# Later read-back of row sums with q and k loaded two pairs ahead, and finished high and low weight parts kept in memory for batches 2 to 4

## The chip, the core and the metric

The kernel runs on one core of a Trainium2 chip. The metric is the time of one execution in microseconds (us), as the device counts it. PE is the matrix engine (TensorE), DVE the vector engine, ACT the scalar engine, POOL is GpSimd, and SP is the engine whose queue issues all of this kernel's DMAs, in program order. Each engine works through its own instruction list in order. A waiting instruction holds up everything behind it on that engine; on SP a waiting DMA issue holds up all later DMAs.

## What is computed

Attention over 4 batches, 12 heads, 448 rows and 64 columns, and then two dense blocks on the result, all in float32 (shortened from the reference):

```
attn = softmax(causal(q @ k.T / 8)) @ v          # q, k, v: (4, 12, 448, 64)
x    = attn.transpose(0, 2, 1, 3).reshape(4, 448, 768)
gate = sigmoid(causal 5-tap convolution of x with conv_w)
x    = (gate * (x @ w_val)) @ w_out              # both 768 x 768
theta = x @ w_theta
y    = w_tok_r @ (x * cos(theta)) + w_tok_i @ (x * sin(theta))   # mixes the 448 rows
u    = x + y
out  = u + relu(u @ w_ch)
```

The weights and `conv_w` arrive as 64-bit floats, 384 KB for a tile of 128 x 384 numbers, and have to be turned into 32-bit numbers in the kernel.

## The kernel before

**Precision.** PE multiplies in a reduced float32 form, so each operand is split into a high part (the value rounded to that form) and a low part (the remainder). Each product is three matmuls: high x high, low x high, high x low.

**Attention** (`attn_iter`) runs head by head; two heads of one batch form a pair `g`, 24 pairs in all, 6 in a batch. For each head it makes scores in four row blocks (`attn_S`), takes the exponential on ACT with the row sums beside it, transposes the probabilities (`attn_PT`), and for each pair multiplies with v (`attn_AV`). `attn_R` (lines 368 to 381) takes the reciprocal of the row sums on DVE, writes these 896 numbers to DRAM (`rows<-rec`, line 375), and at once issues two loads that read them back, spread over all partitions, into a tile `rb` (`rb<-rows`, line 378). `attn_X1` multiplies the product with `rb` (line 389), and `attn_X2` makes the convolution gate. One head is five steps of a generator; `attn_R(g)` is in the fourth step of a pair's second head, `attn_AV(g)` six steps later, `attn_X(g)` four steps after that. The q and k of pair g + 1 are loaded in the second step of pair g's first head, into two buffers each.

**The dense part** (`dense(b)`) of a batch is four stages of six weight groups (`gemm`, lines 440 to 458): `w_val`, `w_out`, `w_theta`, `w_ch`. A group is 128 output columns: two weight tiles of 128 x 384 (g = 0 and 1) and 18 matmuls of 448 columns. Between `w_theta` and `w_ch` come sine and cosine on ACT, transposes (`ztr`) and the token matmuls (`tok`, line 545). The dense part of batch b runs while the attention of batch b + 1 is interleaved with it; the table `RATE` says how many attention steps go with each dense step. The attention of batch 1 runs alone at the start, and the dense part of batch 4 alone at the end. Two groups of batch 1 are multiplied early (`AHEAD`).

**Weights.** In batch 1 a tile is loaded as raw 64-bit numbers (`load_w` into `cv_raw`, four buffers, for group n + 4 while group n is multiplied), converted by three DVE instructions and one on ACT (`to_f32`, in `stage_w`, for group n + 2), written once to DRAM as one float32 tile of 192 KB (`scratch<-w_raw`, line 210), and split by POOL into high (`pool_hi`, line 104) and low (`pool_lo`, line 107, or DVE, line 110) in `split_w`, for group n + 1. In batches 2 to 4 `stage_w` only reads the 192 KB tile back from `scratch` (`w_raw<-scratch`, line 212, three buffers), and `split_w` splits it again on POOL or DVE into `w_hi` and `w_lo` (three buffers each). `W_DVE` says for each batch and stage which low parts DVE makes.

**Order.** All this is written in one stream; a scheduler then orders each engine's list by its own estimate of when things are ready. An `issue_after` block keeps the instructions in it behind a given one on the same engine.

## Time and profile before

| | before |
|---|---|
| time, median of 3 runs | 846.46 us (843.69 to 851.68) |
| profiled execution: its time | 848.2 us |
| profiled execution: span of the trace | 845.7 us |
| PE busy with matmuls | 732.9 us, 87% of the span |
| PE weight loads | 611.6 us, 72% |
| DVE busy | 521.2 us, 62% |
| POOL busy | 515.9 us, 61% |
| ACT busy | 414.1 us, 49% |
| moved by DMA | 88.28 MB, mean 104 GB/s |
| granted PE clock, mean | 0.938 of full speed |

Busy shares are means over stages with different limits, so the kernel is read by stage: the attention of batch 1 (0 to 126 us of the span), the dense part of batch 1 (126 to 342), of batch 2 (342 to 530), of batch 3 (530 to 718) and of batch 4 (718 to 846). PE carries the work that must be done; what a stage can lose is the time in which PE is idle or runs at the lower of its two clocks (1.2 instead of 2.4 GHz; a granted clock of 1.00 is the higher one).

### The profile page before, as it was taken

How to read it: one execution, taken by the hardware profiler on the slowest of the kernel's cores; microseconds unless marked ns; L12 is line 12 of the kernel's file. 1: busy time of each engine (PE TensorE's matmuls, PEld its weight loads, DVE VectorE, ACT ScalarE, POOL GpSimd, SP SyncE). 2: the span in 40 equal slices, each digit the busy share in tenths (PEclk: the TensorE clock that was granted, in tenths of full speed). 3: DMA queues.
4: the chain of work that ended last, by engine and by line, in shares of the span. 5: the costliest groups of instructions: out<-in, count | busy, mean ns of one | idle time of the engine just before them, and what ended most of it. 6: DMA issues, size and time to landing. Idle time of an engine off the chain costs nothing.

```text
span 845.7 us, 12489 instructions
## 1 busy us (share of the span) xinstructions
PE 732.9 (87%) x3965; PEld 611.6 (72%) x3965; DVE 521.2 (62%) x1161; ACT 414.1 (49%) x982; POOL 515.9 (61%) x589
## 2 busy tenths in 40 slices
PE   6577589888397896999889898989989999999997
PEld 4446358666296785878768786868778787898996
DVE  6775698979878562744747644725637834436641
ACT  6667465545567642435558632525558621125311
POOL 3566559667434656577768745567848348676322
PEclk9879669999599898999989999999989999999999
DMA  9984743768534343444423224345332113433113
GB/s 223 185 146 85 139 89 106 206 174 176 181 91 107 61 119 102 82 125 100 101 57 82 52 69 108 89 118 98 84 92 49 32 49 103 132 112 84 36 31 102
DMA packets 151277, 88.28 MB, mean 104 GB/s; under 512 B 93455, under 2 KB 150317, under 8 KB 151213
## 3 DMA queue, kind: packets, MB, share of 16 engines
q1 hardware_dynamic: 151213, 87.51, 42.8%
q8 instruction: 31, 0.51, 0.3%
q14 instruction: 33, 0.27, 0.1%
HBM read 72.45 MB, written 15.03 MB: 103 GB/s over the span
## 4 chain that ended last, share of the span: by engine, by line
PE 47%; DMA 21%; DVE 18%; issue 4%; ACT 4%; POOL 3%; SPq 2%; ACTq 0%; POOLq 0%; DVEq 0%
PE ps_mm L452 23%; PE ps_mm L545 10%; DMA rows<-rec 7%; PE ps_av L357 4%; DMA w_raw<-scratch 4%; PE ps_tr L334 3%; DMA cv_raw<-in_moe_w_val_dram 3%; DMA cv_raw<-in_moe_w_ch_dram 2%; PE ps_s L313 2%; DMA cv_raw<-in_moe_w_theta_dram 2%; DVE w_raw L159 2%; DVE ps_s L315 2%; PE ps_s L314 2%; DVE gate L415 2%; PE ps_tr L531 1%
## 5 line engine op out<-in xcount | busy, mean ns | idle before, releaser
L104 POOL TENSOR_SCALAR w_hi<-w_raw 128x384 fp32r<-128x384 f32 x188 | 113.6, 605 | 151.1 <-PE ps_mm L452 90.1
L452 PE MATMUL ps_mm<-act_hi,w_lo 128*128 128x448 f32 x432 | 163.0, 378 | 8.3 <-POOL w_lo L107 6.4
L452 PE MATMUL ps_mm<-act_hi,w_hi 128*128 128x448 f32 x432 | 163.6, 381 | 6.5 <-POOL w_hi L104 2.1
L107 POOL TENSOR_TENSOR w_lo<-w_raw,w_hi 128x384 fp32r<-128x384 f32 x146 | 157.2, 1078 | 9.3
L452 PE MATMUL ps_mm<-act_lo,w_hi 128*128 128x448 f32 x432 | 159.9, 370 | 0.0
L115 ACT ACTIVATE prob<-ps_s,negm 112x112 f32<-112x112 f32 x192 | 95.2, 497 | 88.3 <-DVE negm L315 86.4
L315 DVE CUSTOM_DVE_ANT_0 ps_s<-ps_s,mask 112x112 f32<-112x112 f32 x192 | 85.6, 454 | 65.1 <-PE ps_s L314 54.4
L334 PE MATMUL ps_tr<-ident,prob 112*112 112x112 f32 x480 | 85.2, 280 | 19.0 <-ACT prob L115 13.1
L452 PEld LDWEIGHTS ps_mm<-act_hi,w_lo 128*128 128x128 f32 x432 | 82.9, 192 | 19.4 <-POOL w_lo L107 10.1
L452 PEld LDWEIGHTS ps_mm<-act_hi,w_hi 128*128 128x128 f32 x432 | 82.4, 192 | 16.0 <-POOL w_hi L104 4.0
L313 PE MATMUL ps_s<-kk,qs 128*112 128x256 f32 x192 | 74.0, 389 | 20.2 <-ACT prob L115 10.3
L452 PEld LDWEIGHTS ps_mm<-act_lo,w_hi 128*128 128x128 f32 x432 | 82.9, 192 | 5.5
L334 PEld LDWEIGHTS ps_tr<-ident,prob 112*112 112x112 f32 x480 | 59.3, 142 | 34.2 <-ACT prob L115 17.9
L107 POOL TENSOR_TENSOR act_lo<-x2f,act_hi 128x448 fp32r<-128x448 f32 x36 | 44.9, 1247 | 53.9 <-DVE act_hi L464 28.4
L347 ACT COPY pt<-ps_tr 112x448 f32<-112x448 f32 (+2 forms) x120 | 51.4, 441 | 48.3 <-PE ps_tr L334 47.6
L357 PE MATMUL ps_av<-pt,v_raw 112*64 112x336 f32 (+3 forms) x384 | 66.4, 451 | 1.7 <-ACT pt L347 1.3
L314 PE MATMUL ps_s<-klo,qs 128*112 128x256 f32 x192 | 62.8, 339 | 3.3 <-DVE klo L110 3.1
L545 PE MATMUL ps_mm<-wtok_h,zt_h 128*128 128x448 f32 x168 | 64.4, 383 | 0.5 <-ACT zt_h L536 0.4
L545 PE MATMUL ps_mm<-wtok_h,zt_l 128*128 128x448 f32 x168 | 63.6, 379 | 1.4 <-DVE zt_l L110 1.3
L545 PE MATMUL ps_mm<-wtok_l,zt_h 128*128 128x448 f32 x168 | 62.0, 369 | 0.0
L411 POOL TENSOR_TENSOR gate<-gate,tp 128x448 f32<-128x448 f32 x48 | 58.8, 1225 | 2.4
L313 PEld LDWEIGHTS ps_s<-kk,qs 128*112 128x112 f32 x192 | 36.7, 192 | 29.1 <-ACT prob L115 12.3
(101 smaller groups left out, 1518.3 us busy)
## 6 DMA issues: line engine op xcount, KB each, us to landing
w_raw<-scratch SPq DMA_DIRECT2D x144, 192.0 KB, 2.4
scratch<-w_raw SPq DMA_DIRECT2D x48, 192.0 KB, 2.8
q_raw<-in_q_dram SPq DMA_DIRECT2D x48, 112.0 KB, 3.0
k_raw<-in_k_dram SPq DMA_DIRECT2D x48, 112.0 KB, 3.3
v_raw<-in_v_dram SPq DMA_DIRECT2D x24, 224.0 KB, 3.2
rb<-rows SPq DMA_DIRECT2D x48, 112.0 KB, 3.3
out_dram<-o SPq DMA_DIRECT2D x24, 224.0 KB, 2.7
cv_raw<-in_moe_w_val_dram SPq DMA_DIRECT2D x12, 384.0 KB, 4.7
```

Of the source, the lines that this page charges most:

```text
L104: nc.gpsimd.tensor_scalar(out=dst, in0=src, scalar1=1.0, scalar2=0.0, op0=ALU.mult, op1=ALU.add)
L107: nc.gpsimd.tensor_tensor(out=dst, in0=src, in1=f32(hi), op=ALU.subtract)
L115: exps.append(nc.scalar.activation(*args, **kw))
L313: nc.tensor.matmul(pt[:CP, :nn], lhsT=qs[:, cs], rhs=kk[:, :nn], start=True, stop=False)
L314: nc.tensor.matmul(pt[:CP, :nn], lhsT=qs[:, cs], rhs=klo[:, :nn], start=False, stop=True)
L315: ttr = nc.vector.tensor_tensor_reduce(out=pt[:CP, :n], in0=pt[:CP, :n], in1=mask[:, S - n : S], scale=-1.0 / math.sqrt(D), scalar=3.0e38, ...
L334: nc.tensor.transpose(pt[:CP, off : off + CP], prob[i, c][:, kc * CP : (kc + 1) * CP], ident[:CP, :CP])
L347: nc.scalar.copy(t, src)
L357: nc.tensor.matmul(av[g][j * D : (j + 1) * D, kc * CP : S], lhsT=tv[:, j, kc, :], rhs=pT.pop((2 * g + j, kc)), start=kc == 0, stop=kc == N ...
L411: nc.gpsimd.tensor_tensor(out=gt, in0=gt, in1=tp, op=ALU.add)
L452: nc.tensor.matmul(pt[:, :S], lhsT=a[:, kc % KH, :], rhs=x, start=kc == 0 and m == 0, stop=kc == KC - 1 and m == 2,)
L545: nc.tensor.matmul(pt[:, :S], lhsT=a[:, m, :], rhs=w[:, m, :], start=m == 0 and n == 0, stop=m == NZ - 1 and n == 2,)
```

## The change

Two things are changed at once.

*Attention.* `attn_R` now ends with the write of the reciprocals. The read-back is a step of its own (`attn_B`), called in the step of `attn_AV` of the same pair, six steps later, behind the load of v for the pair after the next (`issue_after` on that load). The q and k loads are made two pairs ahead at first (pairs 0, 1 and 2 before the loop), and then for pair g + 3 at the end of pair g, just ahead of `attn_R(g)`; there are still two buffers of each.

*Weights.* In batch 1 the converted tile now overwrites the raw one in place (every second 32-bit word of it), POOL and DVE split it from there into one tile `w_hl` that holds high and low part, and this finished 384 KB tile is what is written to `scratch`. Batches 2 to 4 read it back whole (`fetch_w`, for group n + 3) and split nothing. Raw tiles and finished tiles share eight buffers (`wb`); `w_raw`, `w_hi` and `w_lo` are gone. Raw tiles are loaded for group n + 3 instead of n + 4. The rows of `W_DVE` for batches 2 to 4 are dropped, that of batch 1 stays.

```diff
-W_DVE = ('0010', '1000', '0000', '2111')
+W_DVE = '0010'
-    scratch = dram.tile([NW, 2, P, KH * P], F32, name="scratch")
+    scratch = dram.tile([NW, 2, P, 2 * KH * P], F32, name="scratch")
     def load_w(n, g):
...
-            t = pool.tile([P, CV, 2], I32, tag="cv_raw", name="cv_raw", bufs=4)
+        t = pool.tile([P, CV, 2], I32, tag="wb", name="cv_raw", bufs=8)
...
     def stage_w(n, g):
-        if n >= NW * B:
-            return
-        t = pool.tile([P, KH, P], F32, tag="w_raw", name="w_raw", bufs=3)
-        flat = t.rearrange("p c n -> p (c n)")
         if n < NW:
-            to_f32(flat, bits.pop((n, g)))
-            if B > 1:
-                nc.sync.dma_start(out=scratch[n, g], in_=flat)
-        else:
-            nc.sync.dma_start(out=flat, in_=scratch[n % NW, g])
-        raws[n, g] = t
+            to_f32(bits[n, g][:, :, 0], bits[n, g])

     def split_w(n, g):
-        if n >= NW * B:
+        if n >= NW:
             return
-        t = raws.pop((n, g))
+        t = bits.pop((n, g))[:, :, 0].bitcast(F32).rearrange("p (c n) -> p c n", n=P)
...
-            hi = pool.tile([P, KH, P], F32R, tag="w_hi", name="w_hi", bufs=3)
-            lo = pool.tile([P, KH, P], F32R, tag="w_lo", name="w_lo", bufs=3)
+            hl = pool.tile([P, 2, KH, P], F32R, tag="wb", name="w_hl", bufs=8)
+            hi, lo = hl[:, 0], hl[:, 1]
         pool_hi(hi, t)
...
+        elif B > 1:
+            nc.sync.dma_start(out=scratch[n, g], in_=f32(hl.rearrange("p a c n -> p (a c n)")))
+
+    def fetch_w(n, g):
+        if not NW <= n < NW * B:
+            return
+        hl = pool.tile([P, 2, KH, P], F32R, tag="wb", name="w_hl", bufs=8)
+        nc.sync.dma_start(out=f32(hl.rearrange("p a c n -> p (a c n)")), in_=scratch[n % NW, g])
+        splits[n, g] = (hl[:, 0], hl[:, 1])
...
         nc.sync.dma_start(out=rows.rearrange("h c p -> p h c"), in_=rec)
+        row_at[g] = rows
+
+    def attn_B(g):
...
+            if g + 2 in v_ins:
+                st.enter_context(tc.issue_after(v_ins[g + 2].ins))
+            attn_B2(g, rows)
+
+    def attn_B2(g, rows):
         rb = pool.tile([P, S], F32, tag="m2k", name="rb", bufs=2)
...
             split_w(n + 1, g)
             stage_w(n + 2, g)
-            load_w(n + 4, g)
+            load_w(n + 3, g)
+            fetch_w(n + 3, g)
...
-        if j == 0:
-            load_qk(g + 1, "q")
-            load_qk(g + 1, "k")
...
         if j == 1:
+            load_qk(g + 3, "q")
+            load_qk(g + 3, "k")
             attn_R(g)
...
             attn_AV(g - 1)
+            load_v(g + 1)
+            attn_B(g - 1)
```

**SP's list.** First SP, at the third pair of attention that runs within the dense part of batch 2. Before:

```order
L254 DMA q_raw<-in_q_dram 112x4x64 x2
L212 DMA w_raw<-scratch 128x384
L254 DMA k_raw<-in_k_dram 112x4x64
L375 DMA rows<-rec 112x8x1
L254 DMA k_raw<-in_k_dram 112x4x64
L378 DMA rb<-rows 64x448 x2
L212 DMA w_raw<-scratch 128x384 x7
L262 DMA v_raw<-in_v_dram 112x8x64
```

The same pair on SP in the changed kernel, whose lines 233, 259, 267, 380 and 395 are the weight fetch, the q and k loads, the v load, the write of the sums and their read-back:

```order
L259 DMA q_raw<-in_q_dram 112x4x64 x2
L259 DMA k_raw<-in_k_dram 112x4x64 x2
L233 DMA w_hl<-scratch 128x768
L380 DMA rows<-rec 112x8x1
L233 DMA w_hl<-scratch 128x768 x5
L267 DMA v_raw<-in_v_dram 112x8x64
L395 DMA rb<-rows 64x448 x2
L233 DMA w_hl<-scratch 128x768 x2
```

The read-back has moved from one place behind the write to behind five weight fetches and the v load; the fetches have twice the columns.

**POOL's list.** Now POOL in the second stage (`w_out`) of batch 2, where `act_lo<-x2f` is the low part of the stage's results. Before:

```order
L107 TENSOR_TENSOR act_lo<-x2f,act_hi 128x448
L104 TENSOR_SCALAR w_hi<-w_raw 128x384
L107 TENSOR_TENSOR w_lo<-w_raw,w_hi 128x384 x2
L104 TENSOR_SCALAR w_hi<-w_raw 128x384
L107 TENSOR_TENSOR act_lo<-x2f,act_hi 128x448
L107 TENSOR_TENSOR w_lo<-w_raw,w_hi 128x384
L104 TENSOR_SCALAR w_hi<-w_raw 128x384
L107 TENSOR_TENSOR w_lo<-w_raw,w_hi 128x384
L104 TENSOR_SCALAR w_hi<-w_raw 128x384
L107 TENSOR_TENSOR w_lo<-w_raw,w_hi 128x384
L107 TENSOR_TENSOR act_lo<-x2f,act_hi 128x448
```

The whole of that stage on POOL in the changed kernel, up to the first product with the sine (line 539):

```order
L107 TENSOR_TENSOR x_lo<-xf_72,x_hi 128x448
L107 TENSOR_TENSOR act_lo<-x2f,act_hi 128x448
L104 TENSOR_SCALAR kk<-kk 64x448
L107 TENSOR_TENSOR act_lo<-x2f,act_hi 128x448 x5
L107 TENSOR_TENSOR x_lo<-xf_73,x_hi 128x448
L539 TENSOR_TENSOR z<-z,x2f 128x448 x3
```

No weight is split between the results any more; what is left on POOL waits for ACT and PE only.

**ACT's list.** Last ACT at the start of the sine stage of batch 2 (lines 518 and 519 are sine and cosine, 115 the exponential of attention; each has a table of its own). Before:

```order
L518 ACT_TABLE_LOAD
L518 ACTIVATE z<-z 128x448
L519 ACTIVATE z<-z,halfpi 128x448
L513 ACTIVATE z<-z 128x448
L518 ACTIVATE z<-z 128x448
L519 ACTIVATE z<-z,halfpi 128x448
L505 ACTIVATE z<-ps_mm 128x448
```

The same place in the changed kernel, where sine and cosine have lines 536 and 537:

```order
L536 ACT_TABLE_LOAD
L536 ACTIVATE z<-z 128x448
L537 ACTIVATE z<-z,halfpi 128x448
L115 ACT_TABLE_LOAD
L115 ACTIVATE prob,sums<-ps_s,negm 112x336
L531 ACTIVATE z<-z 128x448
L536 ACT_TABLE_LOAD
L536 ACTIVATE z<-z 128x448
L537 ACTIVATE z<-z,halfpi 128x448
L115 ACT_TABLE_LOAD
```

An exponential now stands between the sines of the first two groups, with a table load on each side. In the whole list there are 8 more table loads than before (35 instead of 27): one pair in batch 1, two in batch 2, one in batch 3.

## Rows read from the trace of the kernel before

**Rows 1.** Busy us (and instructions) of each engine, clock and DMA, by stage.
```profile
0.00:126.00 126.00, 86.50 (x438) 61.75 (x439) 90.53 (x242) 76.44 (x215) 69.87 (x85) 0.81 0.72 144
126.00:342.00 216.00, 176.90 (x961) 145.59 (x961) 159.66 (x339) 115.42 (x269) 133.30 (x143) 0.92 0.50 131
342.00:530.00 188.00, 174.05 (x976) 146.68 (x976) 105.89 (x245) 94.50 (x224) 129.49 (x145) 0.97 0.36 88
530.00:718.00 188.00, 174.93 (x976) 147.63 (x975) 105.69 (x241) 93.08 (x212) 122.23 (x141) 0.97 0.32 77
718.00:846.00 128.00, 120.50 (x622) 109.95 (x620) 59.47 (x97) 34.64 (x64) 61.01 (x78) 0.99 0.30 84
```
**Rows 2.** The same columns for five stretches of 20 us.
```profile
350.00:370.00 20.00, 17.32 (x92) 13.46 (x91) 13.60 (x27) 6.93 (x17) 13.45 (x16) 1.00 0.39 75
410.00:430.00 20.00, 15.03 (x72) 12.13 (x70) 13.10 (x26) 10.54 (x24) 15.15 (x18) 0.91 0.40 93
510.00:530.00 20.00, 16.32 (x93) 13.31 (x91) 7.36 (x20) 5.96 (x18) 10.11 (x12) 0.91 0.42 108
540.00:560.00 20.00, 16.01 (x74) 12.52 (x73) 11.62 (x26) 6.23 (x17) 12.39 (x15) 0.91 0.30 76
600.00:620.00 20.00, 14.28 (x71) 11.84 (x70) 12.66 (x27) 12.21 (x26) 14.96 (x18) 0.87 0.39 92
```
**Rows 3.** Chain that ended last, 410 to 430 us: start, us, what.
```profile
411.02 6.98 DMA rows<-rec
...
419.22 3.46 DMA w_raw<-scratch
422.83 0.52 POOL w_hi L104
...
429.54 0.66 PE ps_tr L531 x4
```
**Rows 4.** Waits: who waited for whom, us in total, times, longest.
```profile
SPq L212 <- POOL w_lo L107: 188.3, 73, 16.3
SPq L378 <- DMA rows<-rec: 153.5, 24, 8.5
...
ACT o L576 <- DMA out_dram<-o: 26.2, 4, 8.6
```
**Rows 5.** Groups: line, engine, shapes, count, busy us, mean ns, idle before.
```profile
L107 POOL TENSOR_TENSOR w_lo<-w_raw,w_hi 128x384 fp32r<-128x384 f32 x146 | 157.2, 1078 | 9.3
L104 POOL TENSOR_SCALAR w_hi<-w_raw 128x384 fp32r<-128x384 f32 x188 | 113.6, 605 | 151.1 <-PE ps_mm L452 90.1 <-DMA w_raw<-scratch 35.0 <-DVE w_raw L159 16.7
L110 DVE TENSOR_TENSOR w_lo<-w_raw,w_hi 128x384 fp32r<-128x384 f32 x42 | 27.7, 662 | 37.3 <-POOL w_hi L104 22.8 <-PE ps_mm L452 11.0 <-PE ps_tr L531 3.5
L518 ACT ACT_TABLE_LOAD x14 | 18.0, 1283 | 0.2
```
**Rows 6.** DMA issues: count, KB each, median us from issue to landing.
```profile
w_raw<-scratch SPq DMA_DIRECT2D x144, 192.0 KB, 2.4
...
cv_raw<-in_moe_w_val_dram SPq DMA_DIRECT2D x12, 384.0 KB, 4.7
```
**Rows 7.** SP's issues in order of time: start, us, what.
```profile
576.09 0.31 SPq L375 DMA_DIRECT2D rows<-rec  x1
```
**Rows 8.** Chain that ended last, three of its pieces: start, us, what.
```profile
279.37 10.61 DMA cv_raw<-in_moe_w_ch_dram
...
576.50 7.98 DMA w_raw<-scratch
...
719.97 47.24 PE ps_mm L452 x232
```
**Rows 9.** Columns of rows 1, for two stretches with much DMA.
```profile
180.00:200.00 20.00, 14.69 (x75) 11.78 (x73) 16.82 (x36) 11.01 (x28) 12.16 (x14) 1.00 0.90 272
718.00:765.00 47.00, 46.57 (x231) 42.66 (x230) 19.89 (x33) 10.93 (x21) 31.46 (x42) 1.00 0.43 123
```
**Rows 10.** Who waited for `cv_raw`: us in total, times.
```profile
  DVE cv_raw L152: 26.1, 17
```

More of the change, by code (lines that the diff above doesn't have):

```diff
@@ L224, in split_w @@
         else:
-            hi = pool.tile([P, KH, P], F32R, tag="w_hi", name="w_hi", bufs=3)
-            lo = pool.tile([P, KH, P], F32R, tag="w_lo", name="w_lo", bufs=3)
+            hl = pool.tile([P, 2, KH, P], F32R, tag="wb", name="w_hl", bufs=8)
+            hi, lo = hl[:, 0], hl[:, 1]
         pool_hi(hi, t)
-        w = int(W_DVE[n // NW][n % NW // KC])
-        (dve_lo if w > g else pool_lo)(lo, t, hi)
-        splits[n, g] = (hi, lo)
+        (dve_lo if int(W_DVE[n // KC]) > g else pool_lo)(lo, t, hi)
+        if B > 1 and n < AHEAD:
+            for a, x in enumerate((hi, lo)):
+                nc.sync.dma_start(
+                    out=scratch[n, g][:, a * KH * P : (a + 1) * KH * P], in_=f32(x.rearrange("p c n -> p (c n)"))
+                )
+        elif B > 1:
+            nc.sync.dma_start(out=scratch[n, g], in_=f32(hl.rearrange("p a c n -> p (a c n)")))
+        splits[n, g] = (hi, lo)
+    def fetch_w(n, g):
+        if not NW <= n < NW * B:
+            return
+        hl = pool.tile([P, 2, KH, P], F32R, tag="wb", name="w_hl", bufs=8)
+        nc.sync.dma_start(out=f32(hl.rearrange("p a c n -> p (a c n)")), in_=scratch[n % NW, g])
+        splits[n, g] = (hl[:, 0], hl[:, 1])
     v_ins = {}
@@ L244 @@
     rbs = {}
+    row_at = {}
     ttr_ins = []
@@ L375, in attn_R @@
         nc.sync.dma_start(out=rows.rearrange("h c p -> p h c"), in_=rec)
+        row_at[g] = rows
+    def attn_B(g):
+        if g not in row_at:
+            return
+        rows = row_at.pop(g)
+        with ExitStack() as st:
+            if g + 2 in v_ins:
+                st.enter_context(tc.issue_after(v_ins[g + 2].ins))
+            attn_B2(g, rows)
+    def attn_B2(g, rows):
         rb = pool.tile([P, S], F32, tag="m2k", name="rb", bufs=2)
@@ L620, in attn_iter @@
             attn_AV(g - 1)
+            load_v(g + 1)
+            attn_B(g - 1)
         if i == B * H:
             attn_X(g - 1)
-        if j == 0:
-            load_v(g + 1)
         seg(4)
         yield
-    load_qk(0, "q")
-    load_qk(0, "k")
+    for name in ("q", "k"):
+        load_qk(0, name)
     setup()
     load_v(0)
+    for name in ("q", "k"):
+        load_qk(1, name)
     attn_T(0)
+    for name in ("q", "k"):
+        load_qk(2, name)
     def attention():
@@ L659 @@
                 stage_w(AHEAD, g)
-                load_w(AHEAD + 2, g)
         if n == 5 * H:
@@ L664 @@
                 stage_w(AHEAD + 1, g)
-                load_w(AHEAD + 3, g)
+                load_w(AHEAD + 2, g)
     if AHEAD:
```

25 lines of the change are left out of this document (12 added, 13 removed).

## The prediction

> **What bounds the kernel now.** I read the stages first [rows 1]. In the dense parts of batches 2 and 3 PE is busy 174.05 and 174.93 of 188 us, while DVE, ACT and POOL have much room (POOL 129.49 and 122.23 us). PE bounds these stages and misses 13.95 + 13.07 = 27.0 us in them. Batch 4 is PE's too: 120.50 of 128 us. The first 342 us are different: PE idles 39.5 us in the first 126 and 39.1 us in the next 216, and DVE is busy 159.66 of those 216.
>
> Next, where the 27.0 us lie. Five stretches of 20 us hold 2.68 + 4.97 + 3.68 + 3.99 + 5.72 = 21.0 us of them [rows 2]. The chain of waits says what happens in one [rows 3]: the write of the row sums is under way from 411.02 to 418.00; then comes the load of a weight tile at 419.22, then POOL's split at 422.83, and PE has its next late work at 429.54. SP could not issue the weight load, because the read-back `rb<-rows` stood ahead of it and waited for the write. SP loses 153.5 us so, in 24 waits of 6.4 us each [rows 4]. The other long wait of SP is for POOL to let go of a `w_raw` buffer (188.3 us). So the weights of these batches come through a narrow pipe: three raw buffers, POOL, three split buffers. POOL's splits in turn wait 90.1 us for PE to free a buffer and 35.0 us for the load [rows 5]. Whenever SP stands still for 7 us, the pipe runs dry.
>
> **The change part by part.** All sums are made against the profiled execution, 848.2 us with a span of 845.7 us; it is 1.7 us above the median of 846.46 us, so I subtract the sum from the median.
>
> *Splits of batches 2 to 4.* 144 high parts and 146 - 38 = 108 low parts leave POOL, 144 x 0.605 + 108 x 1.078 = 203 us, and 36 low parts leave DVE, 36 x 0.662 = 24 us [rows 5]. Neither engine is the bound there, so this time itself is worth nothing; what counts is that no weight passes POOL any more and that the read-back no longer stops SP. Group n + 3 is fetched as group n - 1 frees its buffers, so a tile has at least three groups of lead. A group of 18 matmuls takes 47.24 / 232 x 18 = 3.67 us when PE does nothing else [rows 8], three take 11.0 us, and about 20 us with attention between them. A `w_raw` load of 192 KB takes 2.4 us and a raw tile of 384 KB 4.7 us [rows 6]; a fetch of 384 KB in one piece should lie between. It fits.
>
> *What PE gets back in batches 2 and 3.* Four of the five stretches (all but 510 to 530 us) end at a late weight: 17.4 us, of which I take 15. The fifth ends at ACT, which waits for a buffer of `o` whose output DMA is stuck behind the read-back (26.2 us in four waits in the whole run [rows 4]). Now `rb` takes its buffer of the shared pair six steps later, so `o` has two; of 3.68 us I take 2. The lower clock comes right after these holes: 0.91 and 0.87 of full speed in four of the five stretches and 0.97 over the two stages [rows 1, 2], which is at most 0.03 x 376 = 11 us; some of it falls into the holes themselves, so I take 5. Against that, three of the four new pairs of table loads are in these batches, 3 x 2 x 1.283 = 7.7 us of ACT [rows 5]. ACT is busy 94.5 of 188 us, but in the sine stage transposes wait for it; I charge 2, bounds 0 and 7.7. Sum -20, from -36 (every idle us comes back and 9 us of clock) to -8 (half of what hangs on weights). Of the remaining 6.0 us of holes I take 1 for an emptier POOL and DVE.
>
> *Batch 4.* PE idles 0.4 of 47 us in its pure stretch [rows 9] and 7.5 us in the whole stage, mostly at the sine stage and at the end: -1, bounds 0 and -4. The fetches there need 2 x 393 KB in 3.67 us, 214 GB/s. Nothing of before runs at just this rate, but 272 GB/s were moved at 0.90 of the DMA engines and 123 GB/s at 0.43 [rows 9], both about 290 to 300 at full use. It fits, at about three quarters.
>
> *First 126 us.* Six of the 24 stops of SP are here (one for each pair of batch 1), and q and k now stand two pairs ahead of them. But attention alone is a chain through PE, DVE and ACT with none of them full [rows 1], and the DMAs carry as much as before: 0.72 of their engines. I take -4, bounds -10 and +5.
>
> *Dense part of batch 1.* One hole, near 320 us, is an `o` stuck behind the read-back; I count 6 us for it with its clock. The writes to `scratch` double: 48 x 197 KB = 9.4 MB more, 31 us of all DMA engines at 300 GB/s, where their share is 0.50 over the stage and 0.90 between 180 and 200 us [rows 1, 9]. The raw loads lose a group of lead, and DVE already waits 26.1 us for them [rows 10]. I charge 3, so -3 in all; bounds -15 and +10.
>
> *Strided reads.* POOL now reads the converted tile with every second word skipped. No POOL row is strided. Below, nothing; above, as if the gaps cost what a second operand costs: 44 x (1.078 - 0.605) = 21 us of POOL [rows 5], where it is busy 133.30 of 216 us. I take nothing, since DVE is the fuller engine. The Trainium skill, "GPSIMD Engine Reference", section "Performance pitfalls for Q7 kernels", puts half more on reads whose step is over 8 bytes; here it is 8 bytes exactly, so by it nothing is added either. No run here shows that rule yet.
>
> Sum: -20 - 1 - 1 - 4 - 3 = -29, which gives 846.5 - 29 = 817.5, say 817 us.
>
> **The rivals.**
>
> *1. The fetches come late all the same (half the gain).* SP no longer waits, but a DMA issued just behind the write of the row sums still lands late. A `w_raw` load issued at 576.50, 0.4 us behind such a write at 576.09 [rows 7], took 7.98 us instead of 2.4, and a raw load near another took 10.61 [rows 8, 6]. That is just under the 11.0 us of three bare groups, with twice the bytes. For it: these rows. Against it: with attention between the groups the lead is about 20 us, and the dense part of batch 4, where the lead is shortest, has no such write, since all 24 pairs are done by then. If every second hole stays, the term of batches 2 and 3 is -8 instead of -20, and with batch 1 getting 2 us less: 846.5 - 15 = 831 us. The Trainium skill says the same of the cause: by "DMA: Bandwidth & Descriptors", section "Queues, rings and completion order", descriptors on one DMA engine are consumed in ring order, whichever instruction waited. By that rule an earlier issue behind the write gains little by itself, and only the longer lead helps; the 7.98 us agree with it.
>
> *2. The holes are made again (no change).* PE's list is nearly the same; if z, the exponentials or ACT's new table loads are what PE really waits for next, the holes move by a microsecond and stay. For it: 6.0 us of holes have such causes now. Against it: the other 276 us of the two stages hold the same work and lose only these 6.0 us [rows 1, 2]. About 845 us.
>
> *3. Batch 1 pays more than the others gain (slower).* Place: the 36 raw loads of `w_out`, `w_theta` and `w_ch`. The lead falls from two groups before conversion to one, the writes that wait for POOL stand between them on SP, and DVE converts in order, so each late tile holds up everything on DVE, the fullest engine there. Price: 36 x the added lateness L. The rest gains 26 us, so L = 0.7 us is no change and L = 1.0 us is slower by 1%; at 1.3 us it is 846.5 - 26 + 47 = 867 us. For it: the 26.1 us that DVE waits now [rows 10], and 0.90 of the DMA engines [rows 9]. Against it: 216 us for 22 groups are almost 10 us a group [rows 1], and a raw tile lands in 4.7 [rows 6].
>
> *4. Batch 1 gains as well (much faster).* If q and k, v and the raw loads are what the first 342 us hang on, both bounds fall: 846.5 - 22 - 10 - 15 = 799 us.
>
> **How the numbers follow.** The forecast case (803 to 830 us) gets 0.58, rival 1 0.17, rival 2 0.10, rival 3 0.07, rival 4 0.08. A measurement of this kernel can tell a change of about 1% from none, so faster means under 838 us and slower over 855. The forecast, rival 4 and most of rival 1 are faster: 0.81. Rival 2 and the rest of rival 1 are the same: 0.12. Rival 3 is slower: 0.07. The range of 8 in 10 reaches from 795 (rival 4's case with some room) to 840 (rival 1 with batch 1 costing 9 us more); left out are rivals 2 and 3 and a little of rival 4.
>
> **What the changed profile would show.** SP's wait of its read-back for `rows<-rec` is nearly gone (153.5 us now). No POOL instruction splits weights after some 335 us, and PE does not wait for POOL in the weight matmuls of batches 2 and 3. PE is busy some 97% of these two stages, which shrink from 188 to about 178 us each, at a clock near 0.99. The time from a fetch's issue to its landing is 3 to 5 us, more behind a write of row sums, and PE does not wait for it. Batch 1 still shows DVE as its fullest engine and ends some 5 to 10 us earlier. The prediction is wrong if PE waits for `w_hl<-scratch` (rival 1), if holes of the old size end at ACT or DVE (rival 2), or if DVE's wait for `cv_raw` grows well beyond 26.1 us and batch 1 ends later than now (rival 3).

## The result, and the profile after

The changed kernel takes 809.2 us (median of four runs, 808.0 to 815.8) against 845.5 us before, a ratio of 0.958 with a 95% interval of 0.950 to 0.965. The forecast was 817 us in a range of 795 to 840: the direction and the range hold, and the gain was 36 us where 29 were expected. The profiled execution took 808.0 us, with a span of 805.6 us; it is the fastest of its four, and the profiled execution of before (848.2 us) lies above its median, so the stages below sum to 40.1 us less than before (805.6 for 845.7 us) and not to 36.

The stages of [rows 1], cut at the same points of the program (the cuts stand as far ahead of each batch's first gate product as there), with the same columns:

```profile
0.00:127.60 127.60, 92.79 (x445) 62.97 (x445) 88.11 (x245) 77.55 (x218) 72.72 (x89) 0.80 0.63 149
127.60:327.50 199.90, 176.34 (x962) 145.31 (x963) 164.64 (x338) 117.59 (x271) 131.62 (x134) 0.96 0.69 192
327.50:502.60 175.10, 167.37 (x969) 144.04 (x968) 98.58 (x237) 98.90 (x225) 57.70 (x55) 0.99 0.61 150
502.60:677.20 174.60, 169.19 (x981) 146.09 (x979) 95.83 (x236) 95.88 (x214) 45.04 (x46) 1.00 0.59 139
677.20:805.60 128.40, 119.75 (x613) 108.78 (x613) 42.78 (x72) 34.24 (x65) 15.35 (x13) 0.99 0.48 141
```

The two middle stages went from 188 us each to 175.1 and 174.6, batch 1's dense part from 216 to 199.9; the first and the last stage did not move by more than 1.6 us. POOL fell from 129 and 122 us to 58 and 45 in the middle stages, as its splits are gone.

SP's waits (who waited for whom, us in total, times, longest), which answer to [rows 4]:

```profile
SPq L233 <- PE ps_mm L470: 170.4, 77, 17.1
SPq L226 <- POOL w_hl L107: 85.2, 28, 20.3
...
SPq L395 <- DMA rows<-rec: 10.6, 3, 6.6
```

The read-back (L395) waits 10.6 us instead of 153.5. The fetches (L233) wait for PE to free a buffer, which is what a queue that runs ahead looks like. The DMA issues (count, KB each, median us from issue to landing) and POOL's splits, of [rows 6] and [rows 5]:

```profile
w_hl<-scratch SPq DMA_DIRECT2D x144, 384.0 KB, 3.9
scratch<-w_hl SPq DMA_DIRECT2D x44, 384.0 KB, 3.9
...
cv_raw<-in_moe_w_val_dram SPq DMA_DIRECT2D x12, 384.0 KB, 6.8
```
```profile
L107 POOL TENSOR_TENSOR w_hl<-cv_raw,w_hl 128x384 fp32r<-128x384 f32 x38 | 44.0, 1160 | 2.3
...
L104 POOL TENSOR_SCALAR w_hl<-cv_raw 128x384 fp32r<-128x384 f32 x44 | 30.2, 688 | 28.4 <-PE ps_mm L470 11.5 <-DVE cv_raw L159 10.2 <-issue 3.2
...
L536 ACT ACT_TABLE_LOAD x18 | 23.1, 1283 | 0.3
```

A fetch lands after a median of 3.9 us, no fetch shows among PE's waits of batches 2 to 4, and the table loads ahead of a sine rose from 14 to 18, as foretold. The late landings that rival 1 rests on are there all the same: of the 95 fetches between 339 and 681 us, the 36 that were issued while a write of row sums was under way took 4.1 to 11.4 us to land (median 9.0), the other 59 took 2.8 to 7.5 us (median 3.6). The lead covers them, so no wait of PE ends at one. All 95 together:

```profile
DMA to landing us min/median/max: 2.8/4.8/11.4
```

### The profile page after: what moved, and what is told of

It reads as the page before. It is cut to its first block, busy times and chain, and to the rows that moved or that the text cites. A ratio compares the mean times of both kernels' runs of the same rounds, so it can differ in the third digit from the quotient of the medians.

```text
span 805.6 us, 11976 instructions
## 1 busy us (share of the span) xinstructions
PE 725.4 (90%) x3965; PEld 607.2 (75%) x3965; DVE 489.9 (61%) x1125; ACT 424.2 (53%) x990; POOL 322.4 (40%) x337
## 4 chain that ended last, share of the span: by engine, by line
PE 51%; DVE 18%; DMA 10%; ACT 9%; POOL 5%; issue 5%; SPq 0%; POOLq 0%; DVEq 0%; ACTq 0%
PE ps_mm L470 29%; PE ps_mm L563 10%; PE ps_av L362 3%; PE ps_tr L339 3%; DVE gate L432 2%; DMA tok_bits<-in_moe_w_tok_i_dram 2%; DVE cv_raw L155 2%; PE ps_s L318 2%; DMA out_dram<-o 2%; DVE ps_s L320 2%; DMA cv_raw<-in_moe_w_out_dram 2%; DVE cv_raw L152 2%; DVE cv_raw L159 2%; PE ps_s L319 2%; DMA cv_raw<-in_moe_w_ch_dram 2%
## 5 line engine op out<-in xcount | busy, mean ns | idle before, releaser
L470 PE MATMUL ps_mm<-act_hi,w_hl 128*128 128x448 f32 x864 | 272.0, 377 | 5.0 <-POOL w_hl L107 1.9
L470 PEld LDWEIGHTS ps_mm<-act_hi,w_hl 128*128 128x128 f32 x864 | 162.7, 190 | 22.6 <-POOL w_hl L107 2.8
L470 PE MATMUL ps_mm<-act_lo,w_hl 128*128 128x448 f32 x432 | 160.1, 371 | 0.0
L339 PE MATMUL ps_tr<-ident,prob 112*112 112x112 f32 x480 | 82.5, 278 | 12.6 <-ACT prob L115 7.9
L470 PEld LDWEIGHTS ps_mm<-act_lo,w_hl 128*128 128x128 f32 x432 | 82.1, 190 | 5.7
L470 PE MATMUL ps_mm<-x_hi,w_hl 128*128 128x448 f32 x264 | 79.6, 369 | 1.5 <-DVE hf L507 1.0
L362 PE MATMUL ps_av<-pt,v_raw 112*64 112x448 f32 (+3 forms) x384 | 64.9, 446 | 1.6 <-DVE klo L110 1.2
L107 POOL TENSOR_TENSOR x_lo<-xf,x_hi 128x448 fp32r<-128x448 f32 x23 | 30.1, 1308 | 68.9 <-ACT x_hi L411 68.3
L362 PEld LDWEIGHTS ps_av<-pt,v_raw 112*64 112x64 f32 x384 | 29.6, 147 | 37.0 <-issue 20.7
L539 POOL TENSOR_TENSOR z<-z,x2f 128x448 f32<-128x448 f32 x18 | 21.0, 1165 | 89.3 <-ACT z L536 89.2
```

Source lines behind the costliest of these rows:

```text
L107: nc.gpsimd.tensor_tensor(out=dst, in0=src, in1=f32(hi), op=ALU.subtract)
L339: nc.tensor.transpose(pt[:CP, off : off + CP], prob[i, c][:, kc * CP : (kc + 1) * CP], ident[:CP, :CP])
L362: nc.tensor.matmul(av[g][j * D : (j + 1) * D, kc * CP : S], lhsT=tv[:, j, kc, :], rhs=pT.pop((2 * g + j, kc)), start=kc == 0, stop=kc == N ...
L470: nc.tensor.matmul(pt[:, :S], lhsT=a[:, kc % KH, :], rhs=x, start=kc == 0 and m == 0, stop=kc == KC - 1 and m == 2,)
L539: (nc.vector if Z_DVE[b] else nc.gpsimd).tensor_tensor(out=t, in0=t, in1=x2f[e], op=ALU.mult)
```

## Experiments

All twelve runs stand in this table, with the kernel before and the changed one. A stage runs from one batch's first gate product (`hf`) to the next one's in the profiled execution. That is one execution: runs of one kernel differ by up to 8 us (808.0 to 815.8 for the changed one), so a few us in one stage prove little, and a pattern over several kernels more (that of run 3, 820.6 us, is the fastest of its five). The runs were timed in groups, each beside new runs of the kernel before, whose medians lie between 843.1 and 846.5 us; so the ratios compare better than the medians. The last column is the median time from the issue of a raw weight load to its first conversion step, for the last 36 loads, worked out from the timelines of SP and DVE.

| kernel | median us | ratio to before (95%) | start | dense 1 | dense 2 | dense 3 | dense 4 | raw lead |
|---|---|---|---|---|---|---|---|---|
| before | 845.5 | 1 | 131.6 | 222.3 | 189.1 | 178.7 | 124.0 | 4.8 |
| changed | 809.2 | 0.958 (0.950, 0.965) | 133.2 | 206.2 | 176.2 | 165.2 | 124.7 | 8.0 |
| 1 attention half | 823.7 | 0.973 (0.966, 0.979) | 134.7 | 210.3 | 178.7 | 168.1 | 124.4 | 5.0 |
| 2 weights half | 819.5 | 0.967 (0.961, 0.973) | 129.2 | 214.3 | 181.4 | 167.7 | 125.5 | 6.5 |
| 3 later read-back only | 827.4 | 0.977 (0.970, 0.984) | 130.9 | 218.9 | 177.7 | 166.7 | 124.4 | 5.6 |
| 4 read-back put back | 824.9 | 0.974 (0.969, 0.980) | 134.8 | 213.7 | 178.6 | 168.3 | 125.6 | 6.6 |
| 5 q, k one pair ahead | 810.1 | 0.961 (0.957, 0.965) | 128.0 | 213.3 | 177.4 | 166.8 | 125.9 | 7.9 |
| 6 tiles written twice | 819.5 | 0.971 (0.966, 0.976) | 134.6 | 222.5 | 172.0 | 165.7 | 124.6 | 11.7 |
| 7 before, raw lead 3 groups | 844.3 | 1.002 (0.999, 1.004) | 132.1 | 222.1 | 184.0 | 177.2 | 125.5 | 5.0 |
| 8 dense conversion | 810.4 | 0.962 (0.957, 0.966) | 132.4 | 213.0 | 175.4 | 165.9 | 126.4 | 5.5 |
| 9 half of each tile written | 822.7 | 0.971 (0.966, 0.976) | 138.4 | 216.7 | 175.4 | 166.5 | 124.2 | 5.5 |
| 10 six buffers | 828.0 | 0.979 (0.973, 0.984) | 127.1 | 227.8 | 177.6 | 164.3 | 124.5 | 4.8 |
| 11 six buffers, old attention | 833.9 | 0.985 (0.981, 0.989) | 121.0 | 236.2 | 181.8 | 167.5 | 125.4 | 5.1 |
| 12 theta's low parts on POOL | 812.3 | 0.960 (0.956, 0.963) | 136.6 | 208.9 | 177.3 | 165.9 | 124.5 | 9.0 |

### Which half brings what (1 to 5)

**1, the attention half alone.** The kernel before with these edits:

```diff
         nc.sync.dma_start(out=rows.rearrange("h c p -> p h c"), in_=rec)
+        row_at[g] = rows
+
+    def attn_B(g):
...
+    def attn_B2(g, rows):
         rb = pool.tile([P, S], F32, tag="m2k", name="rb", bufs=2)
...
-        if j == 0:
-            load_qk(g + 1, "q")
-            load_qk(g + 1, "k")
...
+            load_qk(g + 3, "q")
+            load_qk(g + 3, "k")
             attn_R(g)
...
             attn_AV(g - 1)
+            load_v(g + 1)
+            attn_B(g - 1)
         if i == B * H:
             attn_X(g - 1)
-        if j == 0:
-            load_v(g + 1)
...
```

> The kernel before with the attention half alone: the read-back of row sums issued later, behind the load of v, and q and k two pairs ahead; the weights of batches 2 to 4 are still loaded as float32 and split on POOL and DVE. Theory S (SP's stop makes the holes): without the stop the weight loads are issued in time, so most of the 27 us that PE idled in the dense parts of batches 2 and 3 comes back, 15 to 20 us, and batch 1's dense part shortens by 8 to 16 us too, because its raw loads stand in the same queue: 845 - 18 - 12 = 815 us. Theory P (the pipe of three raw buffers, POOL and three split buffers makes them): the holes of batches 2 and 3 stay, at most 6 us of them go, and what is left is batch 1's: 830 to 840 us.

**2, the weights half alone.** The changed kernel with all of these edits undone, so that against the kernel before these stay:

```diff
...
+    def fetch_w(n, g):
...
             split_w(n + 1, g)
             stage_w(n + 2, g)
-            load_w(n + 4, g)
+            load_w(n + 3, g)
+            fetch_w(n + 3, g)
...
```

> The changed kernel with the attention half undone: the read-back right behind the write of the row sums again, q and k one pair ahead; finished weight tiles are kept and fetched three groups ahead. Theory S with enough lead: SP still stops for some 6.4 us at each pair, but a fetch now has three groups, some 20 us, so the holes of batches 2 and 3 are gone all the same (their dense parts 177 and 166 us, within 4), and only batch 1 stays long (220 us, within 5): about 825 us. Theory P: the same, since the pipe is gone. Rival 1 of the prediction (a stop of 7 us and a slow landing eat the lead): the dense parts of batches 2 and 3 stay at 185 us or more, 835 to 845 us in all. If batch 1's dense part is short here as well, at 206 us, then it is not SP's stop that made it long, but the weights' handling.

**3, the read-back alone.** As 1, without the lines on `load_qk`:

```diff
...
             attn_AV(g - 1)
+            load_v(g + 1)
+            attn_B(g - 1)
         if i == B * H:
             attn_X(g - 1)
-        if j == 0:
-            load_v(g + 1)
```

> The kernel before with one edit: the read-back of row sums issued six steps later, behind the load of v; q and k one pair ahead as before, weights as before. If the read-back's place is what the attention half is worth, this gives the same time as the attention half (within 4 us). If the earlier q and k are what counts in the first stages, it stays 5 us or more above it, with the difference ahead of 346 us.

**4, the read-back put back**, alone, in the changed kernel:

```diff
...
             attn_AV(g - 1)
-            load_v(g + 1)
-            attn_B(g - 1)
         if i == B * H:
             attn_X(g - 1)
+        if j == 0:
+            load_v(g + 1)
```

> The changed kernel with one edit undone: the read-back is issued right behind the write of the row sums again; q and k stay two pairs ahead and the weights are fetched. If the stop of SP costs nothing once fetches have three groups of lead, the dense parts of batches 2 and 3 stay at 176 and 165 us, and at most batch 1's grows from 206 us towards 222: 809 to 825 us. If the stop costs in batches 2 and 3 too, they grow by 4 us or more each.

**5, q and k put back**, alone, in the changed kernel:

```diff
+        if j == 0:
+            load_qk(g + 1, "q")
+            load_qk(g + 1, "k")
...
-            load_qk(g + 3, "q")
-            load_qk(g + 3, "k")
             attn_R(g)
...
```

> The changed kernel with one edit undone: q and k are loaded one pair ahead again; the read-back stays later and the weights stay fetched. In the four runs so far the first stage (to the first gate product of batch 1) took 134.7 and 134.8 us with q and k two ahead and 130.9 and 129.2 us with one ahead. If the two extra pairs that are loaded at the start cost these 4 us and bring nothing once the read-back is out of the way, this is 3 to 5 us faster than the changed kernel: 804 to 807 us. If the early q and k are what frees batch 1's dense part (it was 8.6 us shorter with them in the kernels without fetched weights), that part grows from 206 to 211 us or more and the time is 810 to 815 us.

*What they say of batches 2 and 3.* Of 367.8 us in the two dense parts, the later read-back alone takes away 23.4 (run 3), the attention half 21.0 (run 1), the weights half alone 18.7 (run 2), the whole change 26.3. So run 1 came out as theory S said in these stages, while its time, 823.7 us, lies between the two theories. The theory that SP's stop makes the holes holds, and the narrow pipe alone makes none: in run 3 weights still go through three raw buffers, POOL and three split buffers, and the holes are gone. But the pipe is needed for the stop to hurt: in run 2 SP still stops at every pair (its wait for the row sums is 130.8 us in 24), and PE's long waits are gone too. Two causes in series: taking either away is enough. That is why the medians don't add: 846 x 0.0231 = 19.5 us for the read-back and 28.0 us for the weights make 47.5 us, and both together (run 5) bring 33.2.

The old read-back still costs 2 to 4 us in batch 2 when weights are fetched (runs 2 and 5, 181.4 and 177.4; run 4 and the changed kernel, 178.6 and 176.2). The buffer of `o` that the prediction named has a part in it: in run 2 PE waits 3.1 us in one piece for ACT's copy into `o` in that stage, in run 5 not at all. ACT's wait for the buffer over the whole run, in run 2 and then in run 5:

```profile
ACT o L582 <- DMA out_dram<-o: 38.2, 8, 10.7
```
```profile
ACT o L594 <- DMA out_dram<-o: 11.5, 5, 3.4
```

*What they say of q and k.* In three pairs of kernels that differ in nothing else (1 and 3, 4 and 2, changed and 5), loading them two pairs ahead lengthens the start: 134.7, 134.8 and 133.2 us with it against 130.9, 129.2 and 128.0 without. Batch 1's dense part is shorter with it in the same pairs, though by very different amounts: 210.3, 213.7 and 206.2 us against 218.9, 214.3 and 213.3. The whole kernel doesn't show a gain from it: 0.958 (0.950 to 0.965) with, 0.961 (0.957 to 0.965) without. The earlier q and k can be left out; that they are the worse choice was not shown.

### Do the fetches come late? (10 and 11)

The rival was that a stop and a slow landing eat up the lead. With six shared buffers instead of eight a fetch has two groups of lead, not three. Run 10 is the changed kernel with this edit alone, run 11 that of run 2 with the same edit.

```diff
...
-        t = pool.tile([P, CV, 2], I32, tag="wb", name="cv_raw", bufs=8)
+        t = pool.tile([P, CV, 2], I32, tag="wb", name="cv_raw", bufs=6)
...
-        hl = pool.tile([P, 2, KH, P], F32R, tag="wb", name="w_hl", bufs=8)
+        hl = pool.tile([P, 2, KH, P], F32R, tag="wb", name="w_hl", bufs=6)
```

> The changed kernel with six shared weight buffers instead of eight. In batch 1 a raw tile then finds a free buffer later. Theory: the raw loads are issued a median 8.0 us before their conversion in the changed kernel and 4.8 us in the kernel before, in which DVE waits 17.8 us for them instead of 5.4 in the dense part of batch 1. If buffers make that difference, the lead falls to about 5 us here, DVE's wait rises to 15 us or more and batch 1's dense part from 206 to 213 us or more. In batches 2 and 3 a fetch has about two groups of lead instead of three. Without SP's stop that is enough: within 4 us of 176 and 165 us each. In all 813 to 822 us. Rival 1 of the prediction (slow landings behind the write of row sums eat the lead): batches 2 and 3 grow by 6 us or more each, 825 to 835 us.

> As the run before, six shared buffers, but with the attention half undone as well: the read-back right behind the write, q and k one pair ahead. With eight buffers this kernel took 819 us and its dense parts of batches 2 and 3 were 181 and 168 us. If the holes of those batches need both SP's stop of 6.4 us and a short lead, they come back here: 185 us or more and 173 us or more, 832 to 842 us in all, 10 us or more above the run with six buffers alone. If a fetch is late for another reason, or two groups are lead enough, it stays at 819 to 826 us.

In run 11 SP stops for the row sums as of old, 72.1 us in 12 between 355 and 700 us, and fetches have the short lead. These are PE's waits of the same stretch; the first two lines are the longest on PE, the last one is all that it waits for a fetch:

```profile
PE ps_tr L537 <- DVE z L526: 3.6, 4, 1.4
PE ps_mm L551 <- ACT zt_h L542: 2.8, 3, 2.3
...
PE ps_mm L458 <- DMA w_hl<-scratch: 0.6, 1, 0.6
```

So the theory behind the expectation of run 11, that the holes come back with a short lead, is wrong: batches 2 and 3 took 181.8 and 167.5 us, as with eight buffers. A group takes 181.8 / 24 = 7.6 us in batch 2 there, two groups 15.2. A stop of 72.1 / 12 = 6.0 us with a landing of 4.0 us (the median there) is less than that, and so is the latest landing in these stages, 12.0 us behind a write of row sums. Rival 1 is out, although both times fall near what was said for it: run 10's 828.0 us lies in rival 1's range and run 11's 833.9 us in that of the holes, but in both it is batch 1 that grew, and batches 2 and 3 together differ from those of the kernels with eight buffers by at most 0.5 us (runs 10 and changed, 11 and 2). What differs from the kernel before, which also asked some two groups ahead (three raw and three split buffers), is that there POOL stood between: its splits waited 35.0 us for loads [rows 5], and whatever POOL had to do next for PE or ACT waited behind them. Now only SP waits, and nobody is behind it. This last step is read from the rows; no run separates it.

The six buffers cost 19 us all the same, all of it in batch 1, where raw tiles share them (next section). There the start is 6 us shorter, as 10 raw tiles are begun in it and not 12, and the dense part is 22 us longer. In that part of run 10 SP's raw loads wait 40.0 us for a buffer until the write of a finished tile has landed (3.4 us in the changed kernel), and PE waits 15.6 us for POOL's splits (3.1 us).

### Batch 1: raw loads, writes and strides (6 to 9)

**7, a group less lead, in the kernel before.**

```diff
-            load_w(n + 4, g)
+            load_w(n + 3, g)
...
```

> The kernel before with one edit: raw weight tiles of batch 1 are asked for three groups ahead instead of four, as the change does. Rival 3 of the prediction: each of the 36 loads is 0.7 us or more later for the conversion, 25 us or more in batch 1's dense part, 870 us. The forecast: 1 to 3 us slower, 847 to 850 us. If the loads are late because SP stands still and not because they are asked for late, nothing changes: within 2 us of 846.

No change (1.002, 0.999 to 1.004). The lead counted in groups is not what sets when a load is issued: in the kernel before a load came a median of 4.8 us ahead of its conversion, with a group less 5.0 us. So the lead did not follow the number of groups. What it follows shows in the last column of the table: with four buffers and SP not stopped it is 5.0 and 5.6 us (runs 1 and 3), with eight and SP stopped 6.5 and 6.6 us (runs 2 and 4), with eight and SP not stopped 8.0 and 7.9 us (changed and 5). The first two ask four groups ahead, the other four three. DVE's waits for raw loads in batch 1's dense part, before and changed:

```profile
DVE cv_raw L152 <- DMA cv_raw<-in_moe_w_ch_dram: 8.4, 7, 4.8
...
DVE cv_raw L152 <- DMA cv_raw<-in_moe_w_out_dram: 6.4, 2, 3.8
...
DVE cv_raw L152 <- DMA cv_raw<-in_moe_w_theta_dram: 3.0, 4, 1.6
```
```profile
DVE cv_raw L152 <- DMA cv_raw<-in_moe_w_out_dram: 2.7, 2, 2.5
DVE cv_raw L152 <- DMA cv_raw<-in_moe_w_ch_dram: 2.7, 2, 2.5
```

17.8 us became 5.4. With six buffers (run 10) the lead is 4.8 us, that of the kernel before, DVE waits 16.4 us again, and the stage takes 227.8 us. The buffers are what counts here, as expected; the size was underestimated (7 us or more expected, 22 in the profile), and not all of it is the lead's, as SP's and PE's waits of run 10 show.

**6, every finished tile written twice.**

```diff
...
-            nc.sync.dma_start(out=scratch[n, g], in_=f32(hl.rearrange("p a c n -> p (a c n)")))
+            for s in (scratch, again):
+                nc.sync.dma_start(out=s[n, g], in_=f32(hl.rearrange("p a c n -> p (a c n)")))
```

> The changed kernel, which also writes each finished tile of batch 1 (groups 2 to 23) a second time, to another place in memory that nothing reads: 44 x 393 KB = 17.3 MB more, almost twice the 9.4 MB that the change added. The prediction charged 3 us for its writes and the lost lead together. If writes cost by volume as charged, this is 3 to 6 us slower than the changed kernel, 812 to 815 us, all of it in batch 1's dense part. If the DMA engines have room there (share 0.71 over the stage), it is within 2 us. If the raw loads queue behind the writes, it is 10 us or more slower and DVE's waits for the raw loads grow from 5 to 15 us or more.

10 us slower than the changed kernel, with 16 us more in batch 1's dense part. A raw theta tile landed 7.0 us after its issue instead of 4.5, and DVE, which is full between 191 and 231 us in the changed kernel, is idle a third of that time in this one (columns as above; the changed kernel first):

```profile
191.00:211.00 20.00, 13.11 (x59) 9.53 (x58) 19.41 (x41) 12.46 (x29) 12.06 (x13) 0.98 0.77 212
211.00:231.00 20.00, 18.46 (x99) 14.77 (x98) 19.64 (x35) 12.08 (x22) 11.45 (x13) 0.94 0.74 236
```
```profile
191.00:211.00 20.00, 11.47 (x36) 7.34 (x36) 13.48 (x21) 5.90 (x12) 9.00 (x9) 0.74 1.04 274
211.00:231.00 20.00, 14.01 (x59) 10.18 (x60) 13.65 (x26) 8.06 (x13) 7.99 (x10) 0.74 0.87 320
```

DVE is busy 13.48 and 13.65 us, with the DMA engines at 1.04 and 0.87. So the DMA engines have no room for another 17.3 MB there. But the sign that the third expectation named did not come: DVE waits 6.5 us for raw loads in batch 1's dense part (5.4 in the changed kernel), and their lead is 11.7 us. Between 191 and 231 us DVE's longest wait is for ACT's step of the conversion (4.0 us in six), and PE waits 10.8 us for POOL's splits. By which of these steps the writes make the stage longer is not shown.

**9, half of each tile written**, which should have priced the 9.4 MB that the change itself added.

```diff
...
-            nc.sync.dma_start(out=scratch[n, g], in_=f32(hl.rearrange("p a c n -> p (a c n)")))
+            nc.sync.dma_start(out=scratch[n, g], in_=f32(hi.rearrange("p c n -> p (c n)")))
...
-        nc.sync.dma_start(out=f32(hl.rearrange("p a c n -> p (a c n)")), in_=scratch[n % NW, g])
+        for a in range(2):
+            nc.sync.dma_start(out=f32(hl[:, a].rearrange("p c n -> p (c n)")), in_=scratch[n % NW, g])
```

> The changed kernel, which writes only the high half of each finished tile (192 KB, as much as the kernel before wrote) and fetches that half twice, so that the product with the low weight parts in batches 2 to 4 uses the high parts in their place; the work of every engine and the bytes fetched stay. It tells what the doubled writes cost. Writing 17.3 MB more made batch 1's dense part 16 us longer. If the cost goes by volume, the 9.4 MB that the change added cost 9 us: 800 us. If the DMA engines have room at the changed kernel's volume and the cost begins only above it, this is within 3 us of 809 us.

13 us slower, with less to write: a miss of both expectations. It doesn't price the writes, because the order of work on DVE came out differently with it: 35 raw tiles are begun ahead of the first `z` product of theta, 31 in the changed kernel. PE waited 12.1 us in one piece for that product, as the kernel before had done (13.2 us) and the changed kernel had not. What the doubled writes cost stays open; run 6 makes it likely that it is more than nothing.

**8, a dense tile for the converted weights.**

```diff
...
-            to_f32(bits[n, g][:, :, 0], bits[n, g])
+            t = pool.tile([P, KH, P], F32, tag="w_raw", name="w_raw", bufs=4)
+            to_f32(t.rearrange("p c n -> p (c n)"), bits[n, g])
+            bits[n, g] = t
...
```

> The changed kernel, but the conversion writes a dense float32 tile of its own (four buffers; the shared buffers fall from eight to six) instead of going back into every second word of the raw tile, so POOL and DVE split from dense reads. In the changed kernel POOL's high part rose from 605 to 688 ns and its low part from 1078 to 1160, and DVE's last conversion step from 677 to 742 ns. If the stride makes these longer, they fall back to 605, 1078 and 677 ns here, DVE has 3 us less to do in batch 1, and the time is 0 to 4 us shorter: 805 to 809 us. If it is the fuller memory traffic that made them longer, they stay where they are and so does the time, 807 to 811 us.

POOL's high part took 623 ns, its low part 1081, DVE's last step 725:

```profile
L107 POOL TENSOR_TENSOR w_hl<-w_raw,w_hl 128x384 fp32r<-128x384 f32 x38 | 41.0, 1081 | 2.0
L159 DVE SCALAR_TENSOR_TENSOR w_raw<-cv_raw 128x384 int32<-128x384 int32 x48 | 34.8, 725 | 5.0 <-ACT cv_raw L158 4.8
...
L104 POOL TENSOR_SCALAR w_hl<-w_raw 128x384 fp32r<-128x384 f32 x44 | 27.4, 623 | 66.1 <-DVE w_raw L159 34.6 <-PE ps_mm L472 24.9 <-issue 3.1
```

The low part falls back to 1081 (1160 with the stride), the high part most of the way. But 1078 and 605 ns of the kernel before are means over all batches. In batch 1's dense part alone its dense reads took 1136 and 652 ns, and in run 6, strided as well as the changed kernel, the two took 1117 and 642. So a stride costs at most some 80 ns here, and part of that, if not all, is the company that POOL has. In time nothing shows, 810.4 and 809.2 us, but the run also changes the buffers, so its time is no price of the stride alone.

### Is DVE the bound of batch 1? (12)

```diff
-W_DVE = '0010'
+W_DVE = '0000'
```

> The changed kernel with one constant changed: the six low weight parts of theta that DVE makes in batch 1 go to POOL. In batch 1 DVE is busy some 19.5 of 20 us between 151 and 251 us, POOL 12 to 16. If DVE bounds this stretch, 6 x 0.66 = 4 us leave it and the time falls by 2 to 5 us: 804 to 807 us. If the raw loads or PE bound it, no change, within 2 us of 809; if POOL's 1.16 us for each comes on the path of the theta weights, 2 us or more slower.

0.960 (0.956 to 0.963), no change that can be seen. 4 us of work taken off DVE in a stretch in which it is busy 19.4 of 20 us did not shorten it. That it is full there does not mean that every us on it counts. What may count instead is the order, that is, what stands ahead of `z`, as follows.

## Why the prediction was right, point by point

**Batches 2 and 3: -21 foretold, -26.3 measured; mechanism right.** The holes ended as said, and the reason was the read-back in front of the weights. By stages, PE idles 7.73 + 5.41 = 13.1 us where it idled 27.0 [rows 1]: 13.9 us back, where 15 + 2 + 1 - 2 = 16 were expected. The clock was undersized: the granted clock is 0.99 and 1.00 instead of 0.97, about 0.02 x 188 + 0.03 x 188 = 9 us, and PE's busy time fell by 6.7 + 5.7 = 12.4 us for practically the same matmuls; the prediction took 5 of a bound of 11. What it left open is what its two reasons, SP's stop and the narrow pipe, are worth apart: they are not two amounts but one chain, and each half alone brings 18.7 to 23.4 of the 26.3 us.

**Batch 4: -1 foretold, +0.7 measured.** Every kernel of the table takes 124.0 to 126.4 us here. PE is the bound, and no weight path could help.

**The first 126 us: -4 foretold, +1.6 measured.** The step that failed is that freeing SP would help here. Moving the read-back alone did next to nothing (130.9 for 131.6 us), and the two pairs loaded ahead cost 4 to 6 us (runs 1 and 3, 4 and 2, changed and 5). The measured value lies within the term's bounds (-10 to +5), nearer to the upper one. Why more loads ahead of time lengthen the stage is not shown; the DMA engines carried 0.63 over it, less than the 0.72 of before.

**Dense part of batch 1: -3 foretold, -16 measured.** This term was off most, and it is the one whose gain is not fully explained. PE's idle time in the stage fell by 39.1 - 23.6 = 15.5 us, so that is where the 16 us are. The attention half alone takes away 12.0 us, the weights half alone 8.0. Three things are in it. The hole near 320 us closed as said: PE waited 5.4 us in one piece there for `x2f`, and 0.6 us in the whole stage of the changed kernel. The part of the charge of 3 us that stood for the lost lead had the wrong sign: the raw loads' lead in time rose from 4.8 to 8.0 us, because buffers and SP's freedom set it, and the number of groups in the code does not (run 7). Rival 3 rested on the same step and falls with it.

The third was not in the prediction at all. In the kernel before PE lost 13.2 us in one piece, to 226 us, to the first `z` product of theta, and the clock was low with it (0.73 between 206 and 226 us, 0.84 in the 20 us after). PE's waits for `z` and for `x2f` in this stage before, and for `x2f` in the changed kernel, in which it has none for DVE's `z`:

```profile
PE ps_tr L531 <- DVE z L520: 15.5, 2, 13.2
...
PE ps_tr L572 <- DVE x2f L583: 5.4, 1, 5.4
```
```profile
PE ps_tr L590 <- DVE x2f L601: 0.6, 1, 0.6
```

The timeline of DVE there (start, us, engine, line), before and changed:

```profile
209.89 0.38 DVE L506 TENSOR_SCALAR z<-z 128x448 f32<-128x448 f32 x1
...
212.56 0.36 DVE L152 TENSOR_SCALAR cv_raw<-cv_raw 128x384 int32<-128x384 uint32 x1 [1.57 <-DMA cv_raw<-in_moe_w_theta_dram]
...
220.56 0.38 DVE L506 TENSOR_SCALAR z<-z 128x448 f32<-128x448 f32 x1
...
224.50 1.55 DVE L520 TENSOR_TENSOR z<-z,x2f 128x448 f32<-128x448 f32 x1
```
```profile
204.33 0.73 DVE L524 TENSOR_SCALAR z<-z 128x448 f32<-128x448 f32 x1
...
210.37 1.12 DVE L538 TENSOR_TENSOR z<-z,x2f 128x448 f32<-128x448 f32 x1 [0.43 <-ACT z L537]
211.41 0.72 DVE L524 TENSOR_SCALAR z<-z 128x448 f32<-128x448 f32 x1
```

From the first step of `z` to its product 14.6 us pass before and 6.0 us after, and the product comes 14 us earlier after (210.37 for 224.50 us). Before, the first steps of the second and third theta stand ahead of the first product (L506 at 220.56 is the third), and 36 raw tiles have been begun by then; after, the product comes right behind its own steps, with 31 begun. Five tiles less are 5 x (0.517 + 0.655 + 0.677) = 9 us of DVE, by the mean times of the three steps before. This order is the scheduler's, and it is in the two lists of instructions: 417 instructions stand ahead of the first product in DVE's list before and 396 after. It could have been read before the run, and PE's wait between 213 and 226 us leads to it. The other runs agree as a pattern: where 35 tiles or more were begun ahead of the first product (runs 1, 3, 7 and 9), PE waited 9.9 to 15.4 us for `z` in this stage (15.5 before); with 34 or fewer, at most 9.0. But the two groups almost touch (9.9 us in run 3, 9.0 in run 4), and an early product does not make the stage short: runs 6, 10 and 11 have 29 to 31 tiles ahead of it and the longest stages of the table, 222.5 to 236.2 us. That this order is worth the rest of the 16 us was not tried by itself: no run changes it and nothing else, so the cause of that part stays open.

**The rivals.** 1 (late fetches) is refuted by runs 10 and 11: its late landings are real (a median of 9.0 us behind a write), but the lead covers them. 2 (holes made again) did not happen: no kind of wait of PE in batches 2 and 3 sums to more than 3.6 us, in the changed kernel as in runs 10 and 11. 3 is refuted by the changed kernel, in which DVE waits less for raw loads and the stage is shorter; run 7 shows that a group less costs nothing even in the kernel before. 4 (batch 1 gains as well, 799 us) was half true, for its dense part and not for its start; the time lies between it and the forecast's 817 us.

**The sum.** That the total came out within 8 us (11 us by the profiled executions) is in part luck: the start missed by 5.6 us to one side, batches 2 and 3 by 5 and batch 1's dense part by 13 to the other, the last of them mostly by something that the prediction did not contain.

**Strides.** Nothing was taken, and no cost in time shows in run 8. The Trainium skill, "GPSIMD Engine Reference", section "Performance pitfalls for Q7 kernels", adds half only for steps above 8 bytes; at exactly 8 the rows show at most 7% on the low part (1160 and 1081 ns) and 10% on the high part (688 and 623 ns), which is not that surcharge.

No run was faster than the changed kernel. Run 5, with q and k left as they were, equals it within what can be measured and is simpler.

## What to carry to other kernels

When a hole needs two things at once (a queue that stops, and a supply too narrow to ride it out), don't price the two cures as a sum: either closes the hole, and the second only brings what else it does. How far ahead a load is made is to be measured as time from issue to use; the number of steps in the code says nothing if a buffer or a blocked queue sets the issue. And when a change lets a scheduler order the work anew, read the lists of the fullest engine for the product that the next engine waits for: a product that stood 21 instructions earlier in DVE's list went with a closed hole of 13 us, half of what the planned part of the change brought in batches 2 and 3; that it was the cause was not tried.

## What the runs showed of the hardware

- In the changed kernel the write of row sums moves 3.5 KB and lands after a median of 7.9 us; a fetch of 384 KB lands after 3.9 us. So size alone does not tell here when a transfer lands. A fetch that is issued while such a write is under way lands late itself, after a median of 9.0 us against 3.6 us for the others of batches 2 and 3. With enough lead that cost nothing; a queue that waits for the write held up all behind it (130.8 us of SP in run 2).

```profile
rows<-rec SPq DMA_DIRECT2D x24, 3.5 KB, 7.9
```

- The DMA engines moved more than the 290 to 300 GB/s at full use that the prediction had worked out: in run 6, between 151 and 171 us, 376 GB/s at a share of 1.05. Between 191 and 211 us of the same run (above) it was 274 GB/s at 1.04. So what full DMA engines move differs by what they move; what makes the difference was not tried.

```profile
151.00:171.00 20.00, 17.01 (x97) 14.91 (x96) 19.11 (x38) 12.21 (x31) 11.16 (x12) 0.96 1.05 376
```

- SP's own issue of a DMA takes unequal time: 1.41 us for a write of a tile at 191.74 us in run 6, and 0.32 for the same at 201.18. Full DMA engines alone do not explain it, as their share is above 1 in the 5 us around either (1.43 and 1.02); what does was not tried.

```profile
191.74 1.41 SPq L228 DMA_DIRECT2D scratch<-w_hl  x1
...
201.18 0.32 SPq L228 DMA_DIRECT2D scratch<-w_hl  x1
```
